# Other products in the first batch's waits, a later second kv, and other buffers and times for one weight

## The chip, the cores and the metric

The kernel runs on one core of a Trainium2 chip. The metric is the device time of one execution in microseconds (us), from the launch to the end of the last instruction; the table below gives the median of three runs. The core's engines are TensorE (PE; its weight loads are PEld), VectorE (DVE), ScalarE (ACT), GpSimd (POOL) and SyncE (SP), which here only issues transfers. Each engine takes its instructions in the order that the program gives it, and waits for the others by semaphores.

## The reference

There are 8 batches of 576 tokens and three stages one behind the other: linear attention with a norm, a gated projection with a causal convolution, and a gated block that mixes the tokens.

```
kv   = k^T v per head (64 x 64);  o = q kv;  x = o / rms(o) * g_norm      # 8 heads of 64: x is 576 x 512
gate = sigmoid(sum over j of conv_w[j] * x shifted by j)                  # 5 taps along the tokens
y    = (gate * (x @ w_val)) @ w_out
h    = gelu(y @ w_in);  u, v = two halves of h (512 each)
v_s  = w_sg @ layernorm(v) + b_sg                                          # 576 x 576 over the tokens
out  = y + (u * v_s) @ w_out2
```

The weights come in as 64-bit floats, the rest in 32 bits.

## The kernel before, in words

**Two passes.** The first pass goes through the batches b = 0 to 7: attention and the gated projection, with y stored to memory (`y_main`, and `y_rest` for the last 64 tokens of each batch, gathered over four batches). The second pass goes through them again: `hv` (the half v of h), `hu`, `sg` (the mixing of tokens) and `wout2`.

**Products.** A large product (`gemm3`) is three products of parts: each operand is kept as a high and a low part, and 4 tiles of 128 rows times 3 pairs make 12 instructions of 128 x 512 into one PSUM bank. Eight banks are shared out in turn (`bank`). A product of plain 32-bit floats (kv, o, the transposes' inputs, the products of `ident` with itself) is two instructions.

**Attention of one batch** (class `Attention`). `load_kv` and `load_q` fetch K, V and Q into single buffers, so a next batch's K and V are fetched when the kv product has read the last. `kv` computes k^T v, `kv_out` copies the 64 x 64 blocks of it to the block diagonal of `kvbd`. `o(t)` multiplies q by it for token tile t (four tiles of 128 and one of 64): ScalarE squares, VectorE sums (line 279), GpSimd raises to the power -1/2 (line 281), VectorE scales (line 284), TensorE transposes (`transpose`, line 299), ScalarE copies the high part and the 32-bit x (lines 303 and 304), VectorE the low part (line 308). `taps` (ScalarE, line 327) and `conv` (VectorE, line 333) compute the gate's argument. `taps` of a feature tile reads all tokens, so it needs all five transposes.

**The start is ordered by hand** (`with tc.manual_schedule()`, lines 667 to 719): each engine gets its instructions in the order of the text. 16 products of `ident` go first on TensorE, while nothing is loaded. The 64-bit weights w_val and the first piece of w_out are converted to high and low parts (`in_turn`, `split`, `wide_parts`: on VectorE lines 127, 128, 120, 129, 124, 167, 169; on ScalarE lines 117 and 162). Then come kv of batch 0 (in two halves, as K and V land in two), its o, sums, scaling and transposes. The conversion of the 20 conv weights (`cw_work`) stands behind the sum of tile 3, the kv of batch 1 in front of the transpose of tile 4. Then come taps, four `val` products, the convolution, and the second piece of w_out.

**All else is ordered by a planner**, which simulates the engines and gives each the instruction that comes first in the text of those ready. Work is put into steps: each b has 8 (`s`), four of `val` and four of `out`; `later(n, fn, rank)` puts work n steps behind, in the order of rank. `behind(marks, fn)` also keeps fn's instructions from being ordered ahead of what had been issued to their engine by that mark. In batches 2 to 5 the 16 pieces of w_in are converted at odd s, behind the mark of three steps before, each piece's load being put two pieces ahead. A piece is 128 x 256; each load goes to one of two buffers "raw", and the steps between go through one buffer "cv". The loads of y for the second pass (`load_piece`, line 426) use the same two "raw" buffers and stand behind the pieces.

**w_out2** has eight such pieces (`w2_pieces`). They go by `background`: one piece per step, from s = 4 of batch 6 on, into the buffers X0h and X0l (x of the even batches), with the load one piece ahead. The second pass keeps v in seven places of K, V and Q (`v_alloc`).

Of the kernel before, what the change touches and what calls it, by code (L numbers as in the profile page):

```python
# [10 lines left out]
F32R = mybir.dt.float32r  # L11
AF = mybir.ActivationFunctionType
# [7 lines left out]
P = 128  # L20
B, S, D, DH = 8, 576, 512, 64
NK = D // P
# [38 lines left out]
def body(ctx, tc, qT, k, v, gcol, w_val, conv_w, w_out, w_in, g_ln, w_sgT, b_sg, w_out2, out, out_r):  # L61
# [8 lines left out]
    def sb(tag, shape, dtype=F32, bufs=1):  # L70
        count[0] += 1
        return pool.tile([P] + shape, dtype, tag=tag, name=f"{tag}_{count[0]}", bufs=bufs)
# [138 lines left out]
    act(sb("st", [3, 8], bufs=5)[:, 0], mhalf, AF.Sigmoid)  # L211

    warm = bank("warm")
    for i in range(16):
        nc.tensor.matmul(warm[:, :P], lhsT=ident, rhs=ident, start=True, stop=True)

    class Attention:
        def __init__(self, b):
# [36 lines left out]
        def kv_out(self):  # L255
            bd = kvbd[self.b % 2]
            for pk, j in self.pk3:
                act(bd[:DH, j, :DH], pk[:DH, :, :DH], AF.Copy)
                if self.b:
                    act(bd[DH:, j, DH:], pk[DH:, :, DH:], AF.Copy)  # L260
                else:
                    nc.vector.tensor_copy(bd[DH:, j, DH:], pk[DH:, :, DH:])  # L262

        def o(self, t, wait=3):
            bd = kvbd[self.b % 2]
# [143 lines left out]
            parts()  # L409

    def w2_pieces():
        p2["w2"] = w2 = [sb(f"X0{i}", [NK, D], F32R) for i in "hl"]
        return [split(w_out2[kt * P:(kt + 1) * P, c:c + WC], w2[0][:, kt, c:c + WC], w2[1][:, kt, c:c + WC])
                for c in range(0, D, WC) for kt in range(NK)]

    def v_alloc():
        vk, vv, vq = sb("K", [5, D], F32R), sb("V", [5, D], F32R), sb("Q", [NK, D], F32R)
        p2["v"] = [(vk[:, 0], vk[:, 1]), (vk[:, 2], vk[:, 3]), (vv[:, 0], vv[:, 1]), (vv[:, 2], vv[:, 3]),
                   (vq[:, 0], vq[:, 1]), (vq[:, 2], vq[:, 3]), (vk[:, 4], vv[:, 4])]

    vnext = [0]

# [235 lines left out]
    def in_turn(*pieces):  # L658

        for p in pieces:  # L660
            p[2]()
        running = [p[3]() for p in pieces]
        while running:
            running = [r for r in running if next(r, running) is not running]


    with tc.manual_schedule():
# [12 lines left out]
        in_turn(wv_pieces[2], wv_pieces[3])  # L680
        wo_pieces[2][0]()
        wo_pieces[3][0]()
        in_turn(wo_pieces[0])
        att.kv(0)
        att.kv(1)
        slots.drain()
        steps = [att.o(t, None) for t in range(5)]
        lows = []
        for t in range(5):
            steps[t][0](ts)  # L690
            if t >= 2:
                steps[t - 2][1]()
                lows.append(steps[t - 2][2]())
            if t == 3:
                cw_work()
            if t == 4:
                lows[0]()
        for t in (3, 4):
            steps[t][1]()
            if t == 4:  # L700
                atts[1].kv(0)
                atts[1].kv(1)
                slots.drain()
            lows.append(steps[t][2]())
            lows[t - 2]()
        lows[3]()
        for m in range(NK):
            att.taps(m)
        moe = Moe(att.xh, att.xl, gate, y_main[0])
        z = [moe.val(m, True) for m in range(NK)]  # L710
        for a in (0, 2):
            att.conv((a, a + 1))
            att.sigmoid(a)
# [10 lines left out]
    for b in range(B):  # L724
# [10 lines left out]
        for s in range(8):  # L735
# [21 lines left out]
                later(0, lambda a=nxt, m=s - 5: a.gates((m, m + 1)), 2)  # L757
            if s == 2:
                later(0, atts[b].rest_parts, 2)
            if b >= 2 and s % 2 and wi_n < len(wi):  # L760
                later(0, lambda w=wi[wi_n][1], m=marks[-3]: behind(m, w), 3)
                if wi_n + 2 < len(wi):
                    later(0, wi[wi_n + 2][0], 4)
                wi_n += 1
            if b == B - 2 and s == 4:
                background(w2_pieces(), 1, 0)
            if b == B - 1:
                if s == 0:
                    v_alloc()
# [136 lines left out]
```

## Time and profile before

| | |
|---|---|
| median of three runs | 777.12 us (776.66 to 777.33) |
| the profiled execution's own time | 778.36 us |
| its span, first to last instruction | 776.5 us |
| TensorE busy | 730.9 us (94%), 4400 instructions |
| VectorE busy | 590.7 us (76%), 1141 |
| ScalarE busy | 348.3 us (45%), 658 |
| GpSimd busy | 153.0 us (20%), 163 |
| mean granted clock of TensorE | 0.965 of full speed |
| moved by transfers | 80.13 MB, 103 GB/s on the mean |

The shares are over the whole span. The profile also cuts the span in 40 slices of 19.4 us, and shows for each engine its instructions in order of time, with the idle time before each and what ended it; and the chain of waits, followed back from the last instruction: at each step to what released it.

### The profile page before, as it was taken

The numbers are of one execution on the slowest core, as the hardware profiler recorded it, in microseconds if no ns is written. First come the engines' busy times: TensorE is split into PE (matmuls) and PEld (weight loads), VectorE is DVE, ScalarE is ACT, GpSimd is POOL, SyncE is SP. The second block draws the span as 40 slices with busy tenths as digits, with TensorE's granted clock in tenths as the row PEclk, the third lists the DMA queues.
The fourth block names the chain that finished last, engine by engine and source line by source line (L and its number), as shares of the span: only waits on it lengthen the run. The fifth ranks groups of instructions, "written<-read, shape, count | busy, mean of one in ns | idle before, by whom it ended". The sixth has DMA issues, their size and how long they took to land.

```text
span 776.5 us, 11579 instructions
## 1 busy us (share of the span) xinstructions
PE 730.9 (94%) x4400; PEld 626.4 (81%) x4400; DVE 590.7 (76%) x1141; ACT 348.3 (45%) x658; POOL 153.0 (20%) x163
## 2 busy tenths in 40 slices
PE   4598899999899999949999999999999999999996
PEld 4486678787778787848988988889899889898896
DVE  7669967897977999857977687776875867877662
ACT  3346455666446567435543343433433424434320
POOL 0405342554352544221101000010000000100000
PEclk8679899999999999979999999999999999999999
DMA  9945035446235211342211132111321221221203
GB/s 294 304 135 184 1 116 177 132 147 206 87 129 203 90 68 44 137 149 86 85 55 64 46 95 82 55 55 56 108 95 55 69 95 38 72 68 41 95 1 108
DMA packets 56199, 80.13 MB, mean 103 GB/s; under 512 B 3664, under 2 KB 29264, under 8 KB 55120
## 3 DMA queue, kind: packets, MB, share of 16 engines
q1 hardware_dynamic: 56144, 79.40, 31.1%
q8 instruction: 34, 0.56, 0.3%
q14 instruction: 21, 0.17, 0.1%
HBM read 60.51 MB, written 18.87 MB: 102 GB/s over the span
## 4 chain that ended last, share of the span: by engine, by line
PE 76%; DVE 10%; DMA 3%; ACT 2%; POOL 2%; issue 1%; DVEq 0%; SPq 0%; POOLq 0%
PE sg L561 15%; PE out L201 12%; PE hu L201 11%; PE hv L452 11%; PE y L201 9%; PE val L201 9%; DVE G L333 5%; PE kv L250 3%; PE o L269 2%; PE xT L299 2%; PE hur L201 1%; POOL st L281 1%; DMA raw<-y_main 1%; DMA raw<-in_w_in_dram 1%; DVE T L284 0%
## 5 line engine op out<-in xcount | busy, mean ns | idle before, releaser
L201 PE MATMUL y<-Z,WO 128*128 128x512 f32 (+1 forms) x480 | 115.7, 388 | 3.8 <-DVE WO L169 3.7
L333 DVE SCALAR_TENSOR_TENSOR G<-X,cw,G 128x576 f32<-128x576 f32 x128 | 99.9, 826 | 10.8 <-ACT G L327 10.8
L201 PEld LDWEIGHTS y<-Z,WO 128*128 128x128 f32 x480 | 83.8, 193 | 20.9 <-DVE WO L169 4.0
L452 PE MATMUL hv<-wiv,X1h 128*128 128x512 f32 x256 | 83.7, 393 | 10.0 <-ACT X1h L429 10.0
L464 POOL TENSOR_TENSOR bmv<-bmv,mhalf 128x1 f32<-128x1 f32 x36 | 21.8, 605 | 348.1 <-DVE bmv L463 337.5
L201 PE MATMUL out<-Z,X0h 128*128 128x512 f32 x256 | 82.9, 389 | 0.0
L201 PE MATMUL hu<-X1h,wiu 128*128 128x512 f32 x256 | 79.5, 391 | 0.0
L281 POOL TENSOR_TENSOR st<-st,mhalf 128x8 f32<-128x8 f32 (+1 forms) x40 | 70.1, 1756 | 30.6 <-DVE st L280 28.1
L441 ACT ACTIVATE T<-T 128x512 f32<-128x512 f32 x68 | 43.1, 633 | 52.2 <-DVE T L438 52.1
L452 PEld LDWEIGHTS hv<-wiv,X1h 128*128 128x128 f32 x256 | 48.1, 189 | 19.9 <-ACT X1h L429 10.4
L201 PEld LDWEIGHTS out<-Z,X0h 128*128 128x128 f32 x256 | 48.1, 188 | 10.0
L201 PEld LDWEIGHTS hu<-X1h,wiu 128*128 128x128 f32 x256 | 46.6, 188 | 8.3
L562 DVE SCALAR_TENSOR_TENSOR T<-sg,gln,cv 128x288 f32<-128x288 f32 x64 | 32.8, 517 | 26.4 <-PE sg L561 26.2
L573 ACT ACTIVATE Z<-T 128x512 fp32r<-128x512 f32 x32 | 20.3, 634 | 67.6 <-DVE T L572 67.6
L452 PE MATMUL hv<-wiv,X1l 128*128 128x512 f32 x128 | 50.1, 392 | 0.0
L201 PE MATMUL hu<-X1l,wiu 128*128 128x512 f32 x128 | 50.1, 391 | 0.0
L201 PE MATMUL out<-Z,X0l 128*128 128x512 f32 x128 | 49.8, 389 | 0.0
L269 PEld LDWEIGHTS o<-kvbd,Q 128*128 128x128 f32 (+1 forms) x320 | 42.4, 193 | 8.3 <-DVE kvbd L262 3.5
L269 PE MATMUL o<-kvbd,Q 128*128 128x128 f32 (+1 forms) x320 | 44.4, 288 | 3.3 <-DVE kvbd L262 3.3
L250 PEld LDWEIGHTS kv<-V,K 128*64 128x64 f32 (+1 forms) x640 | 29.0, 157 | 18.7 <-issue 13.4
L561 PE MATMUL sg<-WV,V 128*128 128x288 f32 x192 | 43.4, 296 | 0.0
L250 PE MATMUL kv<-V,K 128*64 128x64 f32 (+1 forms) x640 | 35.9, 255 | 7.8 <-DMA V<-in_v_dram 7.8
(144 smaller groups left out, 1646.0 us busy)
## 6 DMA issues: line engine op xcount, KB each, us to landing
Q<-in_qT_dram SPq DMA_DIRECT2D x8, 1152.0 KB, 5.6
y_main<-Y SPq DMA_DIRECT2D x8, 1024.0 KB, 3.9
raw<-y_main SPq DMA_DIRECT2D x32, 256.0 KB, 3.1
Y<-y_main SPq DMA_DIRECT2D x32, 256.0 KB, 3.9
out_dram<-Y SPq DMA_DIRECT2D x32, 256.0 KB, 2.3
K<-in_k_dram SPq DMA_DIRECT2D x7, 1024.0 KB, 5.5
V<-in_v_dram SPq DMA_DIRECT2D x7, 1024.0 KB, 9.0
raw<-in_w_in_dram SPq DMA_DIRECT2D x16, 256.0 KB, 5.0
```

The source lines that it names most:

```text
L201: nc.tensor.matmul(ps, lhsT=a[:, kt, msl], rhs=x[:, kt], start=(i == 0), stop=(i == 3 * NK - 1))
L250: nc.tensor.matmul(self.pk[j][h, h], lhsT=self.k[:n, t, js][:, h], rhs=self.v[:n, t, js][:, h], start=(t == 0), stop=(t == 4))
L269: nc.tensor.matmul(po[:n, j * P:(j + 1) * P], lhsT=self.q[:, j, o:o + n], rhs=bd[:, j, :], start=True, stop=True)
L281: nc.gpsimd.tensor_tensor(st[:n, 2], st[:n, 1], mhalf[:n], op=ALU.pow)
L299: nc.tensor.transpose(pt[:, j * P:j * P + n], xo[:n, j * P:(j + 1) * P], ident[:n, :n])
L333: stt(gate[:, m], x32[:, m, j:j + S], cw3[:, m, j:j + 1], gate[:, m], op0=ALU.mult, op1=ALU.add)
L441: act(w, w, AF.Tanh, scale=CG * AG)
L452: nc.tensor.matmul(ps, lhsT=a[:, kt], rhs=p2["wiv"][:, w, kt], start=(i == 0), stop=(i == 3 * NK - 1))
L464: nc.gpsimd.tensor_tensor(mv[:, 3:4], mv[:, 2:3], mhalf[:, 0:1], op=ALU.pow)
L561: nc.tensor.matmul(ps, lhsT=a[:, msl], rhs=w, start=(n == 0), stop=(n == len(mm) - 1))
L562: later(0, lambda: stt(vs[:, sl], ps, gln_s[:, m:m + 1], p2["bsg"][:, sl], op0=ALU.mult, op1=ALU.add))
L573: act(g[:, 0], x, AF.Copy)
```

## The change

In the part ordered by hand: the 16 products of `ident` become a function `busy(n)`; 27 of them stand first, 5 between the two halves of kv of batch 0, 4 behind them, and 4 in front of each of the transposes of tiles 0 to 3. All of kv's copies of batch 0 are made by ScalarE. `cw_work` stands behind these copies, in front of all o. The transpose of tile 4 stands behind `val(0)`, and kv of batch 1 behind `val(1)`. In the planned part: the pieces of w_out2 run as those of w_in do, at odd s of batch 6 and at s = 0 to 3 of batch 7, and go into the buffers of K and V; v is kept in X0h, X0l and Q and the left fifth part of K and V.

```diff
--- before.py
+++ after.py
@@ -211,8 +211,10 @@
     act(sb("st", [3, 8], bufs=5)[:, 0], mhalf, AF.Sigmoid)
 
     warm = bank("warm")
-    for i in range(16):
-        nc.tensor.matmul(warm[:, :P], lhsT=ident, rhs=ident, start=True, stop=True)
+
+    def busy(n):
+        for i in range(n):
+            nc.tensor.matmul(warm[:, :P], lhsT=ident, rhs=ident, start=True, stop=True)
 
     class Attention:
         def __init__(self, b):
@@ -256,10 +258,7 @@
             bd = kvbd[self.b % 2]
             for pk, j in self.pk3:
                 act(bd[:DH, j, :DH], pk[:DH, :, :DH], AF.Copy)
-                if self.b:
-                    act(bd[DH:, j, DH:], pk[DH:, :, DH:], AF.Copy)
-                else:
-                    nc.vector.tensor_copy(bd[DH:, j, DH:], pk[DH:, :, DH:])
+                act(bd[DH:, j, DH:], pk[DH:, :, DH:], AF.Copy)
 
         def o(self, t, wait=3):
             bd = kvbd[self.b % 2]
@@ -409,14 +408,14 @@
             parts()
 
     def w2_pieces():
-        p2["w2"] = w2 = [sb(f"X0{i}", [NK, D], F32R) for i in "hl"]
+        p2["kv"] = [sb(i, [5, D], F32R) for i in "KV"]
+        p2["w2"] = w2 = [t[:, :NK] for t in p2["kv"]]
         return [split(w_out2[kt * P:(kt + 1) * P, c:c + WC], w2[0][:, kt, c:c + WC], w2[1][:, kt, c:c + WC])
                 for c in range(0, D, WC) for kt in range(NK)]
 
     def v_alloc():
-        vk, vv, vq = sb("K", [5, D], F32R), sb("V", [5, D], F32R), sb("Q", [NK, D], F32R)
-        p2["v"] = [(vk[:, 0], vk[:, 1]), (vk[:, 2], vk[:, 3]), (vv[:, 0], vv[:, 1]), (vv[:, 2], vv[:, 3]),
-                   (vq[:, 0], vq[:, 1]), (vq[:, 2], vq[:, 3]), (vk[:, 4], vv[:, 4])]
+        xh, xl, vq = (sb(i, [NK, D], F32R) for i in ("X0h", "X0l", "Q"))
+        p2["v"] = [(t[:, i], t[:, i + 1]) for t in (xh, xl, vq) for i in (0, 2)] + [[t[:, 4] for t in p2["kv"]]]
 
     vnext = [0]
 
@@ -680,34 +679,41 @@
         in_turn(wv_pieces[2], wv_pieces[3])
         wo_pieces[2][0]()
         wo_pieces[3][0]()
+        busy(27)
+        att.kv(0)
+        busy(5)
+        att.kv(1)
+        busy(4)
         in_turn(wo_pieces[0])
-        att.kv(0)
-        att.kv(1)
         slots.drain()
+        cw_work()
         steps = [att.o(t, None) for t in range(5)]
         lows = []
         for t in range(5):
             steps[t][0](ts)
             if t >= 2:
                 steps[t - 2][1]()
+                busy(4)
                 lows.append(steps[t - 2][2]())
-            if t == 3:
-                cw_work()
             if t == 4:
                 lows[0]()
         for t in (3, 4):
             steps[t][1]()
-            if t == 4:
-                atts[1].kv(0)
-                atts[1].kv(1)
-                slots.drain()
-            lows.append(steps[t][2]())
+            if t == 3:
+                busy(4)
+                lows.append(steps[t][2]())
             lows[t - 2]()
         lows[3]()
+        moe = Moe(att.xh, att.xl, gate, y_main[0])
+        z = [moe.val(0, True)]
+        steps[4][2]()
         for m in range(NK):
             att.taps(m)
-        moe = Moe(att.xh, att.xl, gate, y_main[0])
-        z = [moe.val(m, True) for m in range(NK)]
+        z.append(moe.val(1, True))
+        atts[1].kv(0)
+        atts[1].kv(1)
+        slots.drain()
+        z += [moe.val(m, True) for m in (2, 3)]
         for a in (0, 2):
             att.conv((a, a + 1))
             att.sigmoid(a)
@@ -757,13 +763,21 @@
                 later(0, lambda a=nxt, m=s - 5: a.gates((m, m + 1)), 2)
             if s == 2:
                 later(0, atts[b].rest_parts, 2)
-            if b >= 2 and s % 2 and wi_n < len(wi):
+            if b in (2, 3, 4, 5) and s % 2:
                 later(0, lambda w=wi[wi_n][1], m=marks[-3]: behind(m, w), 3)
                 if wi_n + 2 < len(wi):
                     later(0, wi[wi_n + 2][0], 4)
                 wi_n += 1
-            if b == B - 2 and s == 4:
-                background(w2_pieces(), 1, 0)
+            if b == B - 2 and s == 0:
+                w2 = w2_pieces()
+                w2[0][0]()
+                w2[1][0]()
+                w2_n = 0
+            if (b == B - 2 and s % 2) or (b == B - 1 and s < 4):
+                later(0, lambda w=w2[w2_n][1], m=marks[-3]: behind(m, w), 3)
+                if w2_n + 2 < len(w2):
+                    later(0, w2[w2_n + 2][0], 4)
+                w2_n += 1
             if b == B - 1:
                 if s == 0:
                     v_alloc()
```

## Rows read from the trace of the kernel before

**Rows 1.** The page's slices of TensorE: busy tenths and granted clock, 40 equal slices
```profile
PE   4598899999899999949999999999999999999996
...
PEclk8679899999999999979999999999999999999999
```

**Rows 2.** The chain of waits from 0 to 140: start us, us, what
```profile
48.04 3.00 DVE G L333 x4
51.38 7.37 DVE G L333 x11
...
84.71 5.49 PE y L201 x12
```

**Rows 3.** The chain of waits from 270 to 370
```profile
322.95 9.34 PE y L201 x40
...
338.56 3.00 DMA raw<-y_main
```

**Rows 4.** TensorE's timeline from 296 to 366
```profile
342.27 0.79 PE L452 MATMUL hv<-wiv,X1h 128*128 128x512 f32 x1 [10.00 <-ACT X1h L429]
```

**Rows 5.** TensorE's timeline from 0 to 80: start, us, instructions, idle before
```profile
2.27 5.20 PE L215 MATMUL warm<-ident 128*128 128x128 f32 x32 [2.27 <-POOL X L207]
13.64 1.97 PE L250 MATMUL kv<-V,K 128*64 128x64 f32 x32 [6.16 <-DMA V<-in_v_dram]
...
23.61 7.44 PE L269 MATMUL o<-kvbd,Q 128*128 128x128 f32 x40 [3.30 <-DVE kvbd L262]
...
37.57 1.08 PE L299 MATMUL xT<-ident,T 128*128 128x128 f32 x4 [4.01 <-DVE T L284]
...
39.85 5.91 PE L250 MATMUL kv<-V,K 128*64 128x64 f32 x80
45.69 0.69 PE L299 MATMUL xT<-ident,T 64*128 64x64 f32 x4
...
59.07 4.64 PE L269 MATMUL o<-kvbd,Q 128*128 128x128 f32 x39
```

**Rows 6.** VectorE's timeline from 0 to 100
```profile
23.33 0.65 DVE L262 COPY kvbd<-kv 64x64 f32<-64x64 f32 x4
26.36 0.69 DVE L279 TENSOR_REDUCE st<-T 128x8 f32<-128x512 f32 x1 [2.38 <-ACT T L276]
...
35.01 0.18 DVE L128 TENSOR_SCALAR cv<-cv 128x20 f32<-128x20 f32 x1 [2.14 <-ACT cv L117]
...
39.26 0.68 DVE L284 TENSOR_TENSOR T<-o,st 64x512 f32<-64x512 f32 x1
...
41.26 0.75 DVE L308 SCALAR_TENSOR_TENSOR X0l<-xT,gcol,X0h 128x512 fp32r<-128x512 f32 x1 [0.51 <-ACT X L304]
```

**Rows 7.** GpSimd's timeline from 0 to 100
```profile
27.41 6.58 POOL L281 TENSOR_TENSOR st<-st,mhalf 128x8 f32<-128x8 f32 x4 [25.12 <-DVE st L280]
36.96 1.63 POOL L281 TENSOR_TENSOR st<-st,mhalf 64x8 f32<-64x8 f32 x1 [2.98 <-DVE st L280]
```

**Rows 8.** ScalarE's timeline from 0 to 100
```profile
21.35 0.53 ACT L258 ACTIVATE kvbd<-kv 64x64 f32<-64x64 f32 x4
...
46.66 0.48 ACT L304 ACTIVATE X<-xT,gcol 128x256 f32<-128x256 f32 x1
```

**Rows 9.** Two-microsecond windows of TensorE: stretch, busy (instructions), granted clock, DMA share
```profile
82.00:84.00 2.00, 0.00 (x0) 0.92 0.00 0
```

**Rows 10.** The instructions of line 169 from 100 to 350, grouped: median ns, first, last
```profile
L169 DVE TENSOR_TENSOR X0l<-cv x8: 417/426/426, 302.8 to 343.9; 128x256 fp32r<-128x256 f32 x8
```

**Rows 11.** VectorE's timeline, last instructions of pieces of w_in and w_out2
```profile
274.34 0.42 DVE L169 TENSOR_TENSOR wiu<-cv 128x256 fp32r<-128x256 f32 x1 [1.19 <-POOL cv L167]
...
294.11 0.42 DVE L169 TENSOR_TENSOR wiu<-cv 128x256 fp32r<-128x256 f32 x1
...
320.57 0.42 DVE L169 TENSOR_TENSOR X0l<-cv 128x256 fp32r<-128x256 f32 x1
```

**Rows 12.** Ten-microsecond windows of all engines: busy, granted clock, DMA share, GB/s
```profile
310.00:320.00 10.00, 10.00 (x45) 8.03 (x44) 10.00 (x17) 4.30 (x8) 2.09 (x2) 1.00 0.25 101
```

## The prediction

> **What bounds the kernel now.** I read the slices first: TensorE is over 90% busy nearly everywhere, with two weak places, slices 1 to 5 and slice 18, and its clock is low in the same places [rows 1]. A stretch that TensorE fills can't be shortened by this change, which removes no product of the reference; so only those two places can give time. The chain of waits says what holds each. At the start it runs through VectorE: the convolution of the first batch (G, line 333) begins at 48.04 and runs 4 and then 11 instructions without a break, and the first long stretch of TensorE on the chain is at 84.71 [rows 2]. So the start of that convolution sets the time of the first 85 us: what makes it earlier moves all behind it. In slice 18 TensorE ends its last main product at 332.3, and the chain then goes through a load of y_main that is issued only at 338.56 [rows 3]; TensorE's own timeline shows 10.00 us idle before 342.27 [rows 4].
>
> **Why the convolution starts at 48.04.** The timelines of the four engines give it. The conversion of w_out's first piece occupies VectorE until 23.33, where its four copies of kv begin; TensorE's o starts behind the first of them at 23.61 [rows 5, 6]. The squares' sums begin at 26.36 on VectorE [rows 6], GpSimd's powers at 27.41: 4 in 6.58 us, 1.645 each, and the fifth only at 36.96 [rows 7], because VectorE stood 2.14 us in the conversion of the conv weights, which waited for a ScalarE instruction (35.01) [rows 6]. The scaling of token tile 4 is at 39.26 [rows 6]. Its transpose could follow, but 80 products of the second batch's kv stand in front of it in TensorE's queue, 39.85 for 5.91 us at the low clock; the transpose runs at 45.69 [rows 5]. ScalarE copies it at 46.66 [rows 8], takes a tap, and the convolution starts: 2.35 us from 45.69 to 48.04.
>
> **Part 1, conv weights ahead and kv on ScalarE.** The four copies on VectorE (0.65) become four more on ScalarE, where four take 0.53: 21.35 + 1.06 = 22.4 [rows 6, 8]. The weights' conversion now comes on VectorE at 23.33, directly; its six small instructions took 0.19 each behind 35.01 (0.94 for five until 35.95), so 1.2 us, until 24.5. TensorE's o begins at about 21.7, behind the first two copies, and its first tile (8 of 40 in 7.44 us, 1.5 us, at the low clock) is squared by 24.0. So the first sum starts at 24.5 instead of 26.36. The first power follows 1.05 later as now, at 25.55, and nothing now breaks the row of five: 5 x 1.645 = 8.2, so 33.8 where the last now ends at 38.6 [rows 7]. ScalarE's four extra copies are hidden by the conversion on VectorE; without that cover they'd cost 0.5.
>
> **Part 2, token tile 4 and val.** The scaling of tile 4 follows at 33.8, ends 34.5; two remaining low parts of 0.75 at most (41.26) [rows 6], done by 36.0. Two of val(0)'s 12 products need none of these, ten do: 0.2335 each by 40 in 9.34 [rows 3], so 38.3. Now transpose 4 goes, and with the same 2.35 the convolution starts at 40.65 instead of 48.04: **7.4 us** less. VectorE is then late next, as now: its 16 instructions (12.1 us, 48.04 to 60.1 now) and the gating follow unbroken. Beside it TensorE has val(1), kv and val(2), (3): 3 x 2.80 and, with kv at 5.9 as now, 14.3 from 38.8, until 53.1, against 52.7 for the convolution's end; at the full clock it is less. K and V of batch 2 wait for that kv in SP's queue; it ends near 46, as now (45.7), and they are used some 7 us sooner, but behind five tiles of o (39 in 4.64) [rows 5]; I count nothing, and up to 1 us if they land late, since VectorE is the bound there.
>
> **Part 3, idle products.** None is on the path if TensorE's clock is full. 27 products are 54 instructions (16 took 32), 54 x 5.20/32 = 8.8 us, until 11.1; V lands at 13.64 [rows 5]. Five and four more lie in the wait for the second half of V and for kv's copies. The four groups of four stand in front of transposes 0 to 3, each 8 instructions at 4.64/39 = 0.119, 0.95 us, with a transpose 1.6 of each 1.645 us that GpSimd's power takes: just covered. At the low clock they aren't: four transposed tiles took 1.08 at 37.57 [rows 5], 8 products by that 2.16, 3.24 in all. The gain of a full clock in o and kv is hidden behind VectorE and GpSimd; I value it at nothing by itself.
>
> The clock is the open size here. In 82:84 TensorE stood still and the granted clock left full speed [rows 9], and the next 12 products took 5.49 [rows 2] where 12 x 0.2335 is 2.80. In the changed kernel TensorE waits some 2 of 2.5 us between transpose 3 and val(0)'s third instruction; if the clock falls there, the ten products take 10 x 5.49/12 = 4.6 instead of 2.3, and the first part gives 5.1 us instead of 7.4. I take 7.4, since products stand on both sides of that wait, and keep 5.1 as a bound. The Trainium skill, "TensorE: Matmul & The Clock Gate", section "A second HAM failure mode: psum-queue depth-cycling", says that short idle stretches between groups of products can make the clock swing between its levels; that speaks against the idle products holding it at this spot, and by it 5.1 is right. The row of 82:84 agrees for a standstill of 2 us or more; none here shows it for shorter ones.
>
> **Part 4, w_out2.** Its eight pieces now start in batch 6 at s = 4, one per step; from now on at s = 1, 3, 5, 7 and in the first four steps of batch 7, as w_in's pieces run in batches 2 to 5, and into buffers that are free earlier. The same instructions are issued (eight loads, and 6 on VectorE, 2 on ScalarE, 1 on GpSimd each). What they cost is their place: the load of y_main's first tile needs one of the two "raw" buffers and goes when the seventh piece has read its own. The last instruction of the first piece is at 302.8, of the last at 343.9 [rows 10]; the second, caught in the convolution of batch 7, ends at 320.57 [rows 11], so the six behind it come 23.3/6 = 3.9 us apart, with VectorE partly idle. But ahead of 320 VectorE has no room: it is 10.00 of 10.00 busy in 310:320 [rows 12]. Of w_in's pieces three end ahead of a convolution (the third at 274.34) and the fourth, held up by it, at 294.11 [rows 11]; the next, w_out2's first, can't start before that, one buffer "cv" serving all. So I expect two pieces instead of one before the convolution of batch 7, one held up in it, and five behind it instead of six: the load goes one distance, **3.9 us**, sooner. Bounds: 10.0 (the whole wait [rows 4]) and, below nothing, -2.6: a piece takes six instructions of at most 0.43 on VectorE [rows 10], and put ahead of the convolution it can delay the products that follow, if the load then doesn't come sooner. Reuse of X0 and Q for v costs nothing: v is first written after hv, when val of batch 6 has long read X0.
>
> **Sum.** 7.4 + 3.9 = 11.3. The profiled execution took 778.36, its span 776.5 and 1.86 around it: 765.2 + 1.86 = 767.1. The median of the runs, 777.12, is 1.24 below that execution, so I forecast 765.8.
>
> **Rivals.** (a) Main case, 765.8, by itself 762 to 769; the low clock in val(0) gives 768.1. Chance 0.45. (b) The wait at 332 stays: VectorE is full until 320, and five or six pieces still follow. 777.1 - 7.4 = 769.7. For it: [rows 12]. Against: the pieces come three steps sooner. Chance 0.25. (c) The wait goes wholly, because pieces caught in the convolution are done with it: 777.1 - 7.4 - 10.0 = 759.7. For it: VectorE has holes behind 320 that earlier pieces could not have; against: the same full stretch. Chance 0.17. (d) Slower: TensorE's queue becomes the bound of the first batch. If the clock stays low, o ends at 21.7 + 7.4 = 29.1, the four groups and transposes take 4 x 3.24 = 13.0, until 42.1 instead of 33.5; then low parts 2.5, ten products 4.6 and 2.35 put the convolution at 51.5, 3.5 later than now: 780.6. It decides from the point where a group with its transpose takes over 1.645 us for so long that the convolution starts after 48.04. For it: 1.08 per transposed tile at 37.57. Against: 32 idle products took 5.20 at the start, 0.163 each, less than the low clock's 0.27, so they do raise it [rows 5]. Chance 0.04. (e) The change doesn't do what it says at the start: low3 or val(0) come late and the convolution starts within 1.5 us of 48.04 while the wait at 332 stays: 776 to 778, chance 0.04. The remaining 0.05 is for another order of the planned part.
>
> **The numbers.** 765.8; range 757 to 773, which holds (a), (b), and (c) down to 2.7 us below its value, and so some 85 of 100 by these chances, a little less by the unknown order of the planned part. 0.2%, or 1.6 us, is about what a measurement can tell from no change: faster by more 0.92, within 0.04, slower 0.04 (the slow rival).
>
> **What would show it.** The first convolution instruction near 40.6 (part 1 and 2), five powers unbroken from 25.5, val(0) in front of transpose 4 and 12 products in 2.8 with full clock; the first y_main load near 334 less the 7.4, or 327, and an idle time before hv near 6. I am wrong if the convolution starts after 43, if the shift at the start is lost before 100 us, or if TensorE gets idle between 280 and 332.

## The result, and the profile after

The changed kernel takes 770.51 us (median of four runs, 769.15 to 771.06) against 777.23 of the kernel before beside it: 6.7 us less, ratio 0.9913 [0.9895, 0.993]. The profiled execution took 770.46, its span is 768.7, and TensorE's mean granted clock 0.979 instead of 0.965. The forecast was 765.8, the range 757 to 773. The time is that of rival (b), 769.7, and above the main case's own bounds of 762 to 769: the start gave what was expected, w_out2 gave nothing. In the two profiled executions the difference is 7.8 (776.5 to 768.7 of span); the kernel before was profiled in an execution 1.2 above its median.

The page's slices of TensorE, busy tenths and granted clock:

```profile
PE   6897999999899999859999999999999999999997
...
PEclk8998999999999999979999999999999999999999
```

Against [rows 1], the weak place of slices 1 to 5 is smaller, the one of slice 18 is still there (now 17 and 18, as all lies 8 us earlier). The first batch, in TensorE's timeline from 0 to 47 (start, us, instructions, idle before and what ended it):

```profile
2.27 7.81 PE L217 MATMUL warm<-ident 128*128 128x128 f32 x54 [2.27 <-POOL X L207]
14.04 1.97 PE L252 MATMUL kv<-V,K 128*64 128x64 f32 x32 [3.96 <-DMA V<-in_v_dram]
...
22.42 4.83 PE L268 MATMUL o<-kvbd,Q 128*128 128x128 f32 x40 [0.86 <-DMA Q<-in_qT_dram]
...
32.62 0.63 PE L298 MATMUL xT<-ident,T 128*128 128x128 f32 x4
34.02 0.73 PE L201 MATMUL val<-X0h,WV 128*128 128x512 f32 x2 [0.78 <-ACT X0h L302]
35.43 0.51 PE L201 MATMUL val<-X0l,WV 128*128 128x512 f32 x1 [0.68 <-DVE X0l L307]
...
37.97 0.46 PE L298 MATMUL xT<-ident,T 64*128 64x64 f32 x4
...
41.36 3.58 PE L252 MATMUL kv<-V,K 128*64 128x64 f32 x80
```

o takes 4.83 instead of 7.44 and the second kv 3.58 instead of 5.91 [rows 5]: both now run at the full clock. VectorE in the same stretch, then GpSimd:

```profile
24.11 0.18 DVE L653 TENSOR_TENSOR cw<-cv 128x20 f32<-128x20 f32 x1
24.21 0.69 DVE L278 TENSOR_REDUCE st<-T 128x8 f32<-128x512 f32 x1
...
33.38 0.68 DVE L283 TENSOR_TENSOR T<-o,st 64x512 f32<-64x512 f32 x1 [0.24 <-POOL st L280]
33.98 1.39 DVE L307 SCALAR_TENSOR_TENSOR X0l<-xT,gcol,X0h 128x512 fp32r<-128x512 f32 x2
39.83 3.00 DVE L332 SCALAR_TENSOR_TENSOR G<-X,cw,G 128x576 f32<-128x576 f32 x4 [4.45 <-ACT G L326]
```

```profile
25.26 8.08 POOL L280 TENSOR_TENSOR st<-st,mhalf 128x8 f32<-128x8 f32 x5 [22.98 <-DVE st L279]
```

The five powers stand in one row, where four, a hole and one stood before [rows 7], and the convolution starts at 39.83 instead of 48.04 [rows 2]: 8.2 us sooner. At the other place nothing has changed but the time of day. TensorE's timeline from 320 to 340, the chain of waits from 325 to 340, and VectorE's last instructions of pieces (w_in's last, then w_out2's first, second and seventh):

```profile
334.75 0.79 PE L451 MATMUL hv<-wiv,X1h 128*128 128x512 f32 x1 [10.07 <-ACT X1h L428]
```

```profile
330.44 0.02 issue
330.47 0.44 DVE cv L124
330.90 0.02 SPq L425
330.93 0.04 issue
330.97 3.08 DMA raw<-y_main
```

```profile
286.53 0.41 DVE L169 TENSOR_TENSOR wiu<-cv 128x256 fp32r<-128x256 f32 x1
...
295.18 0.42 DVE L169 TENSOR_TENSOR V<-cv 128x256 fp32r<-128x256 f32 x1 [0.61 <-POOL cv L167]
...
312.98 0.41 DVE L169 TENSOR_TENSOR V<-cv 128x256 fp32r<-128x256 f32 x1
...
331.51 0.43 DVE L169 TENSOR_TENSOR V<-cv 128x256 fp32r<-128x256 f32 x1 [0.61 <-POOL cv L167]
```

Every time that [rows 3, 4, 10 and 11] also have is here 7.5 to 7.6 sooner. One piece of w_out2 ends before the convolution of batch 7, the second is caught in it, and the y load goes behind the seventh, as before.

Between these two places the trace moves little, but not evenly. For each kernel below, the windows of two microseconds of TensorE between the first convolution (line 332 here) and the first hv product were summed: idle is 2.00 less busy, low is busy times (1 less granted clock). What is left of the stretch is the same work at the full clock. It is nearly constant, so idle time and clock account for the stretch (one trace of each kernel; us):

```
kernel                         convolution  to hv   idle   low   left
before                            48.04    294.23  20.66  5.10  268.5
changed                           39.83    294.92  19.92  6.07  268.9
e1  idle products gone            43.00    290.05  19.86  1.39  268.8
e2  w_out2 as before              40.34    294.13  20.47  4.58  269.1
e3  y apart                       41.08    284.25   9.63  5.96  268.7
e4  kv in front                   40.33    290.18  20.53  2.33  267.3
e5  transpose 4 first             37.81    293.89  18.23  3.26  272.4
e6  part 1 undone                 47.33    292.01  18.97  4.61  268.4
e7  w_in a batch sooner           39.96    289.64  18.05  2.92  268.7
e9  five idle products            42.78    290.44  17.66  4.62  268.2
f1  e3 + e5, three products       36.65    281.33   6.56  2.93  271.8
e8  e3 + e5, four products        37.67    282.00   8.02  1.72  272.3
f2  f1, Q sooner                  36.17    278.77   5.69  1.54  271.5
f3  before, y apart               47.94    283.94  10.66  5.02  268.3
```

(With transpose 4 first, val(0) stands behind the convolution's start, which adds its 2.8 to the last column.)

Two comparisons in this table show what one trace can differ by with no cause in the edit. The changed kernel, e2, e3 and e7 have the same start, ordered by hand, and yet the convolution starts at 39.83, 40.34, 41.08 and 39.96. In e3 o ran at the low clock, behind the same idle products:

```profile
21.78 7.23 PE L268 MATMUL o<-kvbd,Q 128*128 128x128 f32 x40 [1.81 <-ACT kvbd L261]
```

And behind the start, before, changed, e2 and e3 have TensorE's instructions in the same order, with 4.58 to 6.07 in "low"; 1.6 to 1.7 of it is one fall of the clock near 200, which changed, e2 and e3 have and before has not. So a difference of up to 1.3 at the convolution, or of up to 1.7 in "low", says nothing by itself.

### The profile page after: what moved, and what is told of

It reads as the page before. It is cut to its first block, busy times and chain, and to the rows that moved or that the text cites. A ratio compares the mean times of both kernels' runs of the same rounds, so it can differ in the third digit from the quotient of the medians.

```text
span 768.7 us, 11720 instructions
## 1 busy us (share of the span) xinstructions
PE 734.5 (96%) x4472; PEld 630.0 (82%) x4472; DVE 589.6 (77%) x1137; ACT 348.6 (45%) x662; POOL 152.7 (20%) x163
## 4 chain that ended last, share of the span: by engine, by line
PE 83%; DVE 8%; DMA 4%; POOL 2%; issue 1%; ACT 1%; SPq 0%; DVEq 0%; POOLq 0%
PE sg L560 16%; PE hv L451 13%; PE out L201 12%; PE hu L201 11%; PE val L201 11%; PE y L201 10%; DVE G L332 4%; PE kv L252 3%; PE o L268 3%; PE xT L298 2%; PE hur L201 1%; DMA V<-in_v_dram 1%; DMA Q<-in_qT_dram 1%; POOL st L280 1%; DMA raw<-in_w_in_dram 1%
## 5 line engine op out<-in xcount | busy, mean ns | idle before, releaser
L463 POOL TENSOR_TENSOR bmv<-bmv,mhalf 128x1 f32<-128x1 f32 x36 | 21.7, 603 | 348.2 <-DVE bmv L462 337.5
L201 PE MATMUL out<-Z,K 128*128 128x512 f32 x256 | 82.9, 389 | 0.0
L451 PEld LDWEIGHTS hv<-wiv,X1h 128*128 128x128 f32 x256 | 48.4, 190 | 20.1 <-ACT X1h L428 10.5
L201 PEld LDWEIGHTS out<-Z,K 128*128 128x128 f32 x256 | 48.1, 188 | 10.0
L201 PE MATMUL out<-Z,V 128*128 128x512 f32 x128 | 49.8, 389 | 0.0
L268 PEld LDWEIGHTS o<-kvbd,Q 128*128 128x128 f32 (+1 forms) x320 | 39.4, 180 | 5.8 <-issue 1.8
L201 PE MATMUL val<-X0h,WV 128*128 128x512 f32 x128 | 42.4, 412 | 0.8 <-ACT X0h L302 0.8
L268 PE MATMUL o<-kvbd,Q 128*128 128x128 f32 (+1 forms) x320 | 41.5, 275 | 0.9 <-DMA Q<-in_qT_dram 0.9
L201 PE MATMUL val<-X1h,WV 128*128 128x512 f32 x128 | 41.3, 403 | 0.0
L252 PEld LDWEIGHTS kv<-V,K 128*64 128x64 f32 (+1 forms) x640 | 26.3, 142 | 14.5 <-issue 11.4
```

Source lines behind the costliest of these rows:

```text
L201: nc.tensor.matmul(ps, lhsT=a[:, kt, msl], rhs=x[:, kt], start=(i == 0), stop=(i == 3 * NK - 1))
L252: nc.tensor.matmul(self.pk[j][h, h], lhsT=self.k[:n, t, js][:, h], rhs=self.v[:n, t, js][:, h], start=(t == 0), stop=(t == 4))
L268: nc.tensor.matmul(po[:n, j * P:(j + 1) * P], lhsT=self.q[:, j, o:o + n], rhs=bd[:, j, :], start=True, stop=True)
L451: nc.tensor.matmul(ps, lhsT=a[:, kt], rhs=p2["wiv"][:, w, kt], start=(i == 0), stop=(i == 3 * NK - 1))
L463: nc.gpsimd.tensor_tensor(mv[:, 3:4], mv[:, 2:3], mhalf[:, 0:1], op=ALU.pow)
```

## The experiments

Each kernel was timed in three rounds against the kernel before, which took 776.53 beside e1 to e4, 777.12 beside e5, e6, e7 and e9, and 776.21 beside the others. Where not said otherwise an edit is one to the changed kernel.

**e1: without the idle products behind the first 16.**

```diff
-        busy(27)
+        busy(16)
...
-        busy(5)
...
-        busy(4)
...
-                busy(4)
...
-                busy(4)
```

> The changed kernel without idle products but for 16 at the start, as before the change. Theory A (the clock matters only in val(0)): o and the transposes at the low clock stay hidden behind GpSimd's powers, val(0)'s last ten products take 4.6 instead of 2.5 us, the first convolution starts near 42.4 instead of 39.83, time 772.5 to 773.5. Rival B (the idle products carry the gain at the start): the convolution starts after 45 and the time is 776 or more. Rival C (they do nothing): 39.8 and 770.5.

768.14 (766.91 to 768.67), ratio 0.9889 [0.9867, 0.991]. o runs at the low clock and the convolution starts 3.2 later than in the changed kernel:

```profile
21.83 7.50 PE L268 MATMUL o<-kvbd,Q 128*128 128x128 f32 x40 [2.69 <-ACT kvbd L261]
```

```profile
43.00 3.00 DVE L332 SCALAR_TENSOR_TENSOR G<-X,cw,G 128x576 f32<-128x576 f32 x4 [6.33 <-ACT G L326]
```

The convolution comes near theory A's 42.4, but the time is below that of all three theories. At their own place the products are worth 2 to 3 us, in two parts: o takes 7.50, and val(0), at the low clock too, 5.8 from its first product to transpose 4 instead of 3.95. Over the whole kernel they are worth nothing that can be measured, and if anything less; the intervals overlap. The table says where the rest lies: behind the convolution this kernel loses 1.39 to the low clock, the changed one 6.07, with the same idle time. Of these 4.7, 1.7 is the fall near 200. Another 1.6 stands behind one wait of the changed kernel,

```profile
76.49 4.61 PE L201 MATMUL y<-Z,WO 128*128 128x512 f32 x12 [2.78 <-DVE WO L169]
```

which e1 hasn't: the planner gave it another order there, with o and val in front of most of y.

**e2: w_out2's steps, buffers and v's places as before.**

```diff
-            if (b == B - 2 and s % 2) or (b == B - 1 and s < 4):
-                later(0, lambda w=w2[w2_n][1], m=marks[-3]: behind(m, w), 3)
...
+            if b == B - 2 and s == 4:
+                background(w2_pieces(), 1, 0)
```

> The changed kernel with w_out2's part undone (pieces from step 4 of batch 6 by background, into X0h and X0l). Theory A (an earlier place in the text moves nothing, since every piece stands behind the last piece of w_in in the single cv buffer and behind the convolution): the pieces keep their times, the wait before hv stays 10.0 to 10.1 us, the time is 770.5 within 1.6. Rival B (the part gave some of the 6.7 us, and the start less): 773 to 777, with a wait over 11 us or later pieces.

770.12 (768.96 to 770.43), ratio 0.9912 [0.9887, 0.9936]. VectorE's pieces again, the first two of w_out2:

```profile
295.87 0.42 DVE L169 TENSOR_TENSOR X0l<-cv 128x256 fp32r<-128x256 f32 x1 [0.64 <-POOL cv L167]
...
312.82 0.41 DVE L169 TENSOR_TENSOR X0l<-cv 128x256 fp32r<-128x256 f32 x1
```

They stand within 0.7 us of where they stand in the changed kernel, and the time is the same, as theory A has it. Part 4 is worth nothing that can be measured.

**e3 and f3: the first batch's y loads apart.** They go into buffers of their own instead of the two "raw" ones, in the changed kernel (e3) and in the kernel before (f3).

```diff
-    def load_piece(src, h, l):
+    def load_piece(src, h, l, own=False):
...
-        y = sb("raw", [NK, P], bufs=2)
+        y = tmp(NK * P).rearrange("p (k n) -> p k n", k=NK) if own else sb("raw", [NK, P], bufs=2)
```

> The changed kernel with the first batch's four loads of y for the second pass in the temporary buffers T instead of raw. Theory A (the wait of 10.07 us before hv is the raw buffer alone): the first load is issued before 320, hv follows the products of y without a wait, time 760 to 761.5. Rival B (behind the buffer, ScalarE's and VectorE's queue with w_out2's pieces holds the splitting of y): the load is early, but hv still waits 3 us or more, or a wait as long comes later; 765 to 769.

> The kernel before, with one edit: the first batch's loads of y for the second pass go into a buffer of their own instead of the two that the pieces of w_out2 use. Theory A (the 10 us without work on TensorE before hv are the wait for these buffers and nothing else): the wait at 332 goes, 777.1 - 10.0 = 767.1, between 765.5 and 768. Rival B (VectorE is the bound there, and the pieces of w_out2 are late for the second pass as well): part of the wait comes back before hu or sg, the gain is under 6 us, 771 or more.

e3 758.82 (758.01 to 759.15), ratio 0.9769 [0.9749, 0.979]; f3 765.09 (764.1 to 766.26), ratio 0.9852 [0.9834, 0.987]. TensorE at hv in e3, then in f3:

```profile
323.71 1.79 PE L201 MATMUL y<-Z,WO 128*128 128x512 f32 x7
325.33 0.40 PE L451 MATMUL hv<-wiv,X1h 128*128 128x512 f32 x1
```

```profile
331.88 0.40 PE L452 MATMUL hv<-wiv,X1h 128*128 128x512 f32 x1
```

The wait is gone in both; the last instruction of w_out2's pieces starts at 348.58 in e3, 12 us later than in the changed kernel, and no instruction is seen to wait for it. The gain is more than the 10.07 of the wait: 11.7 between the medians of the changed kernel and e3, 11.1 between those of before and f3. In the traces f3's span is 12.1 less than that of before, 10.0 of it the wait. The rest is the clock behind it. The changed kernel in windows of two microseconds (stretch, busy, granted clock):

```profile
334.00:336.00 2.00, 1.25 (x5) 0.50 0.03 8
336.00:338.00 2.00, 2.00 (x11) 0.50 0.44 129
338.00:340.00 2.00, 2.00 (x6) 0.51 0.85 253
```

Summed as in the table, from hv to the end, the low clock costs 2.60 in the changed kernel, 2.16 in the one before, and 0.00 in e3 and f3. For f3, 10.0 + 2.2 = 12.2. The same buffers hold up hv in both kernels, whatever is done with w_out2's steps.

**e4: the second kv in front of transpose 4, val behind it, as before.**

```diff
+            else:
+                atts[1].kv(0)
+                atts[1].kv(1)
+                slots.drain()
+                steps[t][2]()
...
-        z = [moe.val(0, True)]
-        steps[4][2]()
...
-        atts[1].kv(0)
-        atts[1].kv(1)
...
+        z = [moe.val(m, True) for m in range(NK)]
```

> The changed kernel with the second batch's kv again in front of the transpose of token tile 4 and all val behind it; idle products and conv weights as changed. Theory A (at the full clock the place of kv is worth nothing: 80 products take 3.6 us and start at once behind transpose 3, near 33.3, while val(0) waits for the low parts until 35.4): transpose 4 near 37, convolution at 38.7 to 39.5, time 769.5 to 770.5. Rival B (the move behind val is a main part of the gain): convolution at 43 or later, 774 or more.

766.70 (765.4 to 767.4), ratio 0.9871 [0.9849, 0.9892]. kv in TensorE's timeline:

```profile
34.48 3.58 PE L252 MATMUL kv<-V,K 128*64 128x64 f32 x80
37.98 0.46 PE L298 MATMUL xT<-ident,T 64*128 64x64 f32 x4
```

At the full clock the 80 products take 3.58, and transpose 4 runs behind them at 37.98, as it did behind val(0) at 37.97; the convolution starts at 40.33, 0.5 from the changed kernel, which is within what equal starts differ by. So at the full clock the place of kv is worth nothing by itself; what it is worth at the low clock no run shows. The time missed both theories: the kernel is 3.8 faster, and that comes behind the convolution, where the planner's order is the one of e1: 2.33 of low clock instead of 6.07, without the wait at 76.49 (1.6) and the fall near 200 (1.7).

**e5: transpose 4 in front of val(0).**

```diff
-        z = [moe.val(0, True)]
         steps[4][2]()
+        z = [moe.val(0, True)]
```

> The changed kernel with the transpose of tile 4 in front of val(0) instead of behind it. Theory A (val(0) in TensorE's queue holds up the transpose by 3.9 us and nothing else does): first convolution 13.5 to 14.0 us behind w_out's first piece instead of 17.4, and that passes to the end: 766.5 to 767.5. Rival B (VectorE then waits for val(2) and val(3), which end as late as now): the gating starts only 1 to 2 us sooner, 768.5 to 769.5.

766.43 (764.04 to 767.29), ratio 0.9857 [0.9836, 0.9877]. TensorE:

```profile
24.19 4.83 PE L268 MATMUL o<-kvbd,Q 128*128 128x128 f32 x40 [2.60 <-DMA Q<-in_qT_dram]
...
35.97 0.43 PE L298 MATMUL xT<-ident,T 64*128 64x64 f32 x4 [0.96 <-DVE T L283]
```

o started 1.8 later than in the changed kernel, since Q landed later in this execution, and still the transpose ran 2.0 and the convolution started 2.0 sooner (37.81). From the last instruction of w_out's first piece to the convolution it is 15.4 instead of 17.4, not the 13.5 to 14.0 of theory A, as o was late. Val(0) in front of the transpose is a cost, not a gain. The kernel is 4.1 faster; what is beyond the 2.0 lies behind the convolution, in idle time (1.7 less) and low clock (2.8 less, 6.07 to 3.26).

**e6: part 1 undone** (`cw_work` behind the sum of tile 3, half of kv's copies on VectorE), all else as changed.

```diff
...
+                if self.b:
+                    act(bd[DH:, j, DH:], pk[DH:, :, DH:], AF.Copy)
+                else:
+                    nc.vector.tensor_copy(bd[DH:, j, DH:], pk[DH:, :, DH:])
...
-        cw_work()
...
+            if t == 3:
+                cw_work()
```

> The changed kernel with part 1 undone: the conv weights are converted behind the sum of tile 3, and VectorE makes four of kv's copies. Measured from the last instruction of w_out's first piece on VectorE to the first convolution instruction: 17.4 us in the changed kernel, 25.4 before the change. Theory A (part 1 gives what the powers show, the fifth 4.8 us sooner, less what val(0) hides): 20.5 to 22.2, and, as the planner's order is here the one with w_out's last pieces close together, worth some 4 us, the time 769 to 771.5. Rival B (part 1 gives little, the rest is the clock): 17.4 to 18.5, time 766 to 767.5.

773.98 (772.88 to 775.77), ratio 0.9954 [0.9937, 0.9971]. VectorE's wait for the conversion, and what TensorE does behind it:

```profile
34.14 0.18 DVE L128 TENSOR_SCALAR cv<-cv 128x20 f32<-128x20 f32 x1 [2.44 <-ACT cv L117]
...
47.33 3.00 DVE L335 SCALAR_TENSOR_TENSOR G<-X,cw,G 128x576 f32<-128x576 f32 x4 [5.55 <-ACT G L329]
```

```profile
36.71 0.63 PE L301 MATMUL xT<-ident,T 128*128 128x128 f32 x4 [3.12 <-DVE T L286]
37.18 1.67 PE L217 MATMUL warm<-ident 128*128 128x128 f32 x8
```

The convolution starts at 47.33, 25.0 behind the last instruction of w_out's first piece. That is more than either theory gave part 1, and so is the time: of the 8.2 us 7.5 hang on part 1, as the rest of the start now stands (6.3 against e3, the latest of the equal starts). The hole of 2.44 stops TensorE for 3.12, and behind that its clock is at 0.50 from 38 to 44: eight idle products take 1.67 instead of 1.06, and val(0) too runs at the low clock until 44.

**e7: w_in's pieces one batch sooner** (in batches 1 to 4).

```diff
-            if b in (2, 3, 4, 5) and s % 2:
+            if b in (1, 2, 3, 4) and s % 2:
```

> The changed kernel with w_in's 16 pieces in batches 1 to 4 instead of 2 to 5; w_out2's pieces as changed. Theory A (w_out2's pieces could not come sooner because w_in's last piece, in the same cv buffer, ended only 8 us before): the first piece ends 15 us or more sooner, the seventh before 325, the wait before hv falls under 4 us, time 762 to 766.5. Rival B (VectorE is full ahead of the convolution of batch 7, so six pieces follow it anyway): pieces and wait as now, 769 to 772.

767.9 (765.71 to 771.25), ratio 0.9884 [0.9851, 0.9917]. VectorE's first pieces of w_out2, then TensorE at hv:

```profile
284.66 0.41 DVE L169 TENSOR_TENSOR V<-cv 128x256 fp32r<-128x256 f32 x1
...
294.05 0.42 DVE L169 TENSOR_TENSOR V<-cv 128x256 fp32r<-128x256 f32 x1 [0.63 <-POOL cv L167]
...
310.99 0.41 DVE L169 TENSOR_TENSOR V<-cv 128x256 fp32r<-128x256 f32 x1
```

```profile
329.60 0.80 PE L451 MATMUL hv<-wiv,X1h 128*128 128x512 f32 x1 [6.89 <-ACT X1h L428]
```

Neither theory was met: the first piece ends 10.5 sooner, not 15, the wait is neither under 4 nor as before, and the time, 765.71 to 771.25, can't be told from the changed kernel's. w_in's last piece now ends at 228.40 and leaves the buffer "cv" free, but VectorE starts w_out2's first piece only at 271.26, in the convolution of batch 6: here the buffer no longer holds it back. The trace is the picture that was forecast for part 4: two pieces before the convolution of batch 7, the third caught in it, and the wait shorter by about one distance, 10.07 - 6.89 = 3.2.

**e9: five idle products instead of four in front of the transposes.**

```diff
-                busy(4)
+                busy(5)
```

> The changed kernel with 5 instead of 4 idle products in front of each of the transposes 0 to 3. On TensorE this adds at most 0.2 us per tile (10 x 0.119 + 0.6 against 1.645), but the planner draws another order behind the start: w_out's last two pieces end close together instead of 8.6 us apart. Theory A (the planner's order, not the idle products, is what made the kernel without them faster): the convolution of batch 0 starts as now or up to 0.6 later, TensorE's wait before the y products near 75 goes, time 766 to 767.5. Rival B (the order is worth nothing; idle products cost): 770.5 to 771.5.

767.5 (766.69 to 768.45), ratio 0.9876 [0.986, 0.9891]. The convolution starts at 42.78, 3 later than in the changed kernel (o started at 23.39 and took 6.45, partly at the low clock, as it also did in e3 with four), and yet the kernel is 3 faster: behind the convolution it has 2.3 less idle time and 1.5 less of the low clock. The wait of 2.78 at 76.49 is gone, as theory A has it. One more idle product in the part ordered by hand gives another planned order: in the traces TensorE's differs between 76 and 106, and VectorE's in places up to 224.

**f1, e8, f2: the parts together.** f1 has the y loads apart, transpose 4 first and three idle products; e8 the same with four; f2 is f1 with the load of Q ahead of those of gcol and g_ln.

```diff
-        dma(gcol_s, gcol)
-        dma(gln_s, g_ln)
         cw_work = taps()
         att.load_q()
+        dma(gcol_s, gcol)
+        dma(gln_s, g_ln)
```

> The changed kernel with the first batch's y loads in a buffer of their own, transpose 4 in front of val(0), and 3 idle products instead of 4 in front of each of the transposes 0 to 3. If the parts add up: 770.5 - 11.5 (y apart) - 4.1 (transpose 4 in front) = 754.9; with 3 idle products the planner puts the last two pieces of w_out's second half close together, so theory O (that order is worth about 4.5 us) expects 750.4, 749 to 752.5. Rival T (those gains came from the clock or from chance in the start): 754 to 756.

> As the kernel with y apart, transpose 4 in front and 3 idle products, but with 4 of them as in the change; the planner then draws the order of before. Theory O: 754 to 756.5, 4 to 5 us more than with 3 products, TensorE waiting some 3 us before the first y products and these at the low clock. Rival T: within 1 us of the one with 3 products.

> As the kernel with y apart, transpose 4 in front and 3 idle products, with the load of Q issued ahead of those of gcol and g_ln. Theory Q (o of the first batch waits for Q): Q lands at 19 to 20.5 instead of 22.3, o starts at 21.7 behind kv's copies, the convolution up to 1.5 us sooner: 749 to 750.5. Rival V (VectorE's first sum stands behind the conversion of the conv weights anyway): no difference beyond 0.5 us. Slower only if gcol lands behind the first transpose, near 29.

f1 750.96 (750.44 to 751.52), ratio 0.9674 [0.9659, 0.9689]; e8 753.88 (753.21 to 754.49), 0.9711 [0.9696, 0.9727]; f2 749.82 (748.2 to 751.25), 0.9664 [0.9638, 0.969]. f1 and f2 beat both kernels, f1 by 25.3 and 19.6 us. TensorE where the second half of w_out is first used, in e8 and in f1:

```profile
70.17 1.05 PE L268 MATMUL o<-kvbd,Q 128*128 128x128 f32 x8
73.38 4.61 PE L201 MATMUL y<-Z,WO 128*128 128x512 f32 x12 [2.16 <-DVE WO L169]
```

```profile
75.09 0.40 PE L201 MATMUL val<-X1l,WV 128*128 128x512 f32 x1
75.32 2.73 PE L201 MATMUL y<-Z,WO 128*128 128x512 f32 x11
```

In e8 the planner puts y in front, which waits for VectorE and then runs at the low clock; in f1 val stands there and y follows at full speed. So theory O holds in kind, but its size was too large: 2.9 us between the two medians, not 4 to 5. Of the 1.9 between the two traces, 1.0 is the start, where Q landed later in e8's execution (o at 24.05, in f1 at 23.03), and 1.5 idle time; the clock goes 1.2 the other way, by a fall in f1 near 190. Theory Q failed in part: the load of Q was issued 2.5 sooner, but o still waits for it and starts 0.6 sooner, and the convolution 0.5 (f2, then f1):

```profile
22.45 4.92 PE L268 MATMUL o<-kvbd,Q 128*128 128x128 f32 x40 [0.52 <-DMA Q<-in_qT_dram]
```

```profile
23.03 4.83 PE L268 MATMUL o<-kvbd,Q 128*128 128x128 f32 x40 [2.00 <-DMA Q<-in_qT_dram]
```

In the other traces where o waits for Q, with the load in its old place, it starts between 22.42 and 24.19, so these 0.6 are not shown to be the edit's. Whether f2 is faster than f1 stays open, the runs overlap.

## Why the prediction was right, and where it failed

The range held the time only because it was drawn wide enough for rival (b), which had 0.25: the main case fails by its second term, w_out2, and what happened there is (b)'s own reason, VectorE full and six pieces behind. None of the three signs of being wrong came up: the convolution starts before 43, the shift is kept, and TensorE has 0.2 us without work from 280 to 324. But of the signs of being right one is missing, the idle time before hv near 6.

**Part 1 and 2 as a sum: right.** Forecast 7.4 at the convolution, measured 8.2 (7.0 to 8.2 in the four traces with this start). Each step is found: first sum at 24.21 (24.5 forecast), powers from 25.26 for 8.08 (25.55, 8.2), scaling of tile 4 at 33.38 (33.8), low parts done at 35.4 (36.0), transpose 4 at 37.97 (38.3), the convolution 1.86 behind it (2.35). o started at 22.42, not 21.7, as it waits for Q; that cost nothing here, because the first sum stands behind the conversion of the conv weights on VectorE (24.11).

**Their parts: one mis-sized.** I gave part 1 the 4.8 us by which the last power comes sooner. e6 shows 7.5: 5.0 at the scaling of tile 4 (38.40 there, 33.38 here), and the rest behind it, where its hole lets the clock fall in the idle products, a transpose and val(0). Part 2 was given the rest; e4 shows no gain from kv's place, at the full clock, and e5 that val(0) in front of the transpose costs 2 us or more. The step "now transpose 4 goes" took val(0)'s place for granted: the transpose had its input at 34.1 and stood behind 3.9 us of low parts and products that it doesn't need.

**Part 3: its bound not reached, its price of nothing wrong at its own place.** The 5.1 for a low clock in val(0) was not met: TensorE stood still for 0.78 and 0.68 between transpose 3 and val(0)'s third instruction, and the pairs behind it take 0.62, the full clock. The Trainium skill, "TensorE: Matmul & The Clock Gate", section "A second HAM failure mode: psum-queue depth-cycling", says that short idle stretches between groups of products can make the clock swing; with the idle products the trace does not agree at this spot. Without them it does: in e1 TensorE stood still for 0.40 to 0.78 in front of each transpose and of val(0), and its clock is 0.52 in 34:36. The changed kernel's trace agrees at another place too: from 192 to 200 its TensorE is busy for 1.35, 0.99, 0.82 and 1.25 of each 2.00 us, and then

```profile
200.00:202.00 2.00, 2.00 (x8) 0.51 0.36 119
202.00:204.00 2.00, 2.00 (x10) 0.64 0.03 12
```

which costs 1.7. I had written that no row of the kernel before shows such a fall behind pauses under 2 us. That holds for the rows quoted, not for its trace: there TensorE stood still for 1.54 and for 1.16 before two transposes, and then ran at the low clock,

```profile
68.00:70.00 2.00, 0.63 (x4) 1.00 1.02 285
70.00:72.00 2.00, 1.50 (x6) 0.50 1.01 384
```

So the idle products hold the clock in val(0), which is what the bound had priced. That o's clock is hidden behind VectorE and GpSimd was wrong: in e3, with o at 7.23, the way from w_out's first piece to the convolution is 18.5 instead of 17.4, 1.1 longer. "Nothing by itself" fits the whole kernel's time, but e1, the run that says so, has another planned order behind the start; what the idle products are worth with the order kept, no run shows.

**Part 4: the step that failed** is "two pieces instead of one before the convolution of batch 7". The working itself had w_in's last piece held until after the convolution of batch 6, and w_out2's first unable to start before it; it did not follow that through. Three steps more of lead weren't used while w_in's last piece held the one buffer "cv" until 286.53: w_out2's first piece ends at 295.18 with the lead and at 295.87 without (e2), and VectorE is then full (300:310 holds 10.00 busy). The price of a piece was about right: when w_in is moved instead, the second piece comes before the convolution and the wait falls by 3.2 (e7), against 3.9 by the forecast. The upper bound for this part, 10.0 for the whole wait, was itself too low: the wait carries about 2 us of low clock behind it (e3, f3).

**Not foreseen: the planner's order.** I gave 0.05 to another order. In each experiment that edits the start the stretch to hv changes by its idle time and its low clock, up to 5 us (e1, e4, e9), with no edit there. Not all of that is the order: 1.7 of what e1 and e4 have less of the low clock is the fall near 200, and before, with the changed kernel's order, has no such fall either. The order's own part is seen at the wait of 2.78 and the 1.6 of low clock behind it (76.49), which e1, e4, e9, f1 and f2 don't have. The change itself kept the order of before on TensorE; it has 0.7 less idle time and 1.0 more low clock than before, so 8.2 at the convolution became 7.5 at hv and 7.8 at the end. How much of a kernel's low clock belongs to its order and how much to the one execution that was traced stays open: f1 and f2 have the same planned order, and only f1 loses 2.9 between 180 and 215.

## What to carry to other kernels

When a wait hangs on a shared buffer, ask what holds the buffer at that moment and walk back to the first piece of that queue which is late; here more lead for the pieces behind it moved nothing, while a buffer of the waiter's own took away the whole wait, and the low clock behind it. Before a step is moved ahead on an in-order engine, look at what then stands behind it and could have gone: here the transpose behind val(0). And where a planner orders the rest, measure an edit at its own place and read the stretch behind it as idle time and low clock, since the total mixes the edit with a redrawn order. Compare kernels that should be equal first: here equal starts differed by 1.3 us at the convolution.

## What the runs showed that I had not expected

A pause of TensorE can be paid twice: the 10 us before hv cost another 2.2 to 2.6 at half clock behind them, and the twelve y products behind the wait of 2.16 in e8 take 4.61 where f1 has eleven of them in 2.73. It need not be: pauses of 3.3 to 3.8 us in all between 180 and 215, much the same in every trace, are followed by a fall of the clock in seven kernels and not in the other seven. And a load issued 2.5 sooner (Q in f2) took 10.9 us to land instead of 9.0 in f1, so most of the lead was lost; one trace of each shows it.
